# Gate/up by strip matmuls with early products, P·V ahead of the scores in a pass, and two row blocks of wo loaded before the last V page

## The chip, the cores and the metric

One Trainium2 chip; the kernel runs on one core. The core has a matrix engine (TensorE, PE in the profile; its weight loads are PEld), a vector engine (VectorE, DVE), a scalar engine (ScalarE, ACT), GpSimd (POOL), and SyncE (SP), which here issues every DMA of data. Each engine runs its own instruction stream; they meet at semaphores. The metric is the device time of one execution in microseconds, as the median of several runs.

## The reference

One token (`x`, 512 wide) goes through a grouped-query attention over a long cache and, beside it, through a gated feed-forward block; a scalar gate mixes the two:

```python
def reference(A_x, A_k_cache, A_v_cache, A_wq, A_wo, B_x, B_w_gate, B_w_up, B_w_down, gate_w):
    x = A_x                                              # [1, 1, 512]
    g = sigmoid((x * gate_w).sum(-1, keepdims=True))
    # attention: 32 query heads, 8 key/value heads, 32768 cached positions, head width 128
    q = x @ wq                                           # 512 x 4096
    p = softmax(q k^T * 128 ** -0.5)                     # 4 query heads share one key/value head
    a = (p v) @ wo                                       # 4096 x 512
    b = (silu(x @ w_gate) * (x @ w_up)) @ w_down         # 512 x 1792, 512 x 1792, 1792 x 512
    return g * a + (1 - g) * b
```

All inputs are bfloat16. The caches are 2 x 8 x 32768 x 128 values, 134 MB together.

## The kernel before, in words

**Storage.** SBUF holds three pages of one cache head each (`page`, 64 KB in each of 128 partitions, 8.39 MB in all). Pages 0 and 1 take the K heads in turn, page 2 the V heads. At the start page 2 holds `wq`, `w_gate` and `w_up` instead; at the end page 0 holds `w_down` and `wo`.

**The order of loads (SP, L331 to L357).** All loads of data are issued by SP in one order, and SP waits in that order too: `wq`, `x`, `gate_w`, `w_gate`, `w_up`, K0, K1; then for each j the load of K(j+1) (when its page's transposes are done, `sem_tr`) and of V(j) (V0 when gate/up is done, `sem_pe_h`; each later one when P·V of the head before has read the page, `sem_v_done`). After K7 and V6 come `w_down`, V7 in five pieces (each as V6's rows are used up), and `wo` in five pieces cut by `WO_CUTS` (in row blocks, 32 in all). SP then waits for the result row and stores it.

**Start (PE `emit_q`).** Four small matmuls turn `x` into columns (`xT`). 32 matmuls with one column of `xT` as the stationary operand give q as rows: four strips of the array at once, 512 columns each, into `ps_sc` (L381). Then gate and up: 112 matmuls (L398) whose stationary operand is a 128 x 128 piece of the weights and whose moving operand is one column of `xT`, in a loop of 2 x 7 turns of 8 matmuls; the result is two groups of 14 columns in `ps_c`. Then four matmuls (L410) spread the transposed q, from which VectorE builds `qblk`. VectorE reads q (L608) and transposes it (L613) while gate/up runs.

**Scores (S).** For each head VectorE transposes the K page in 32 units of 128 x 512 words into two slots (L672, `sem_tr`); TensorE works each unit off with 16 columns of q as the moving operand, 8 matmuls per unit (`emit_s`, L436, `sem_sc`). The two engines hand the two slots back and forth. At the end of a head VectorE takes the maximum (`pmax`, L681), GpSimd makes it global (L295), ScalarE forms the exponentials (L557) and rearranges them into `ET` (L570).

**P·V.** `emit_v` has 64 matmuls in four strips (L455) that read V's page; every eighth signals `sem_v_done`. ScalarE copies the result out (L566), four transposes (`emit_reduce`, L469) follow, and VectorE sums the diagonal blocks into `oT`.

**The pass loop.** TensorE has one hardware loop over passes p = 1 to 11. A pass does the scores of head p-1 and then, from pass 2 on, P·V of head p-2 with its reduction (`emit_v(p)`, `emit_reduce(p + 1)`). The order of work is so S0; S1, V0; S2, V1; and so on to S7, V6; then `w_down` (`emit_wd`, L482) and V7; then the output projection (`emit_wide`), and in the last pass the rest of `wo`. `emit_wide` takes the first 20 row blocks of `wo` in four strips of 512 columns (L501) into `ps_w`, and the others as pairs of 256 columns into `ps_c` (`emit_wo`, `emit_rows`, L230). VectorE copies `ps_w` to `part` (L735), two more pairs of matmuls add the strips of `part` into `ps_c`, and VectorE writes the row (L747).

**The gated product.** ScalarE takes the sigmoid of the gate (L543); VectorE forms the products and scales them by 1 - g in `emit_end`, after the scores of the last head (L697, L702, L704). `w_down` needs them.

## Time and profile before

| | |
|---|---|
| time, 3 runs | median 354.25 us (354.12 to 354.78) |
| profiled execution | 354.53 us, span 353.0 us |
| busy, share of the span | PE 51%, PEld 33%, DVE 53%, ACT 26%, POOL 2% |
| read from HBM | 148.11 MB, 420 GB/s over the span |
| longest waits of the DMA queue (SP) | for P·V (L455) 247.5 us, for gate/up (L398) 37.5, for the transposes (L672) 26.4 |
| gate/up, L398 | 15.9 us of matmul, from 18.07 to 41.24 us |
| chain that ended last | DMA 45%, DVE 21%, PE 21%, issue 11% |

The span runs from the first to the last instruction. The chain is followed back from the last instruction to what released it at each step; "issue" is time in which an engine waited for nothing that the profile shows, so its own stream (branches, register work). A line such as `L672 <-DMA ...` gives what ended the idle time of that line's engine. DMA's "us to landing" counts from the issue to the last semaphore signal.

### The profile page before, as it was taken

Reading aid. Unit: us, or ns where it says so; the run is one execution under the profiler, and the core shown is the slowest. Engines: PE = TensorE matmul, PEld = TensorE weight load, DVE = VectorE, ACT = ScalarE, POOL = GpSimd, SP = SyncE. Lnnn points to the kernel's source line nnn. Section 1 sums busy time; section 2 is a strip of 40 time slices with the busy share of each in tenths; the row PEclk is TensorE's granted clock in tenths of the full one; section 3 lists DMA queues with packets and bytes.
Section 4 is the critical chain, followed back from the end, with each engine's and each line's share of the span. In section 5 each row is a group of like instructions: output and inputs, shape, how many; then the busy total and the mean of one; then the engine's idle time right before and its main releaser. Section 6 shows DMA issues by size and latency. Waiting matters only on the chain.

```text
span 353.0 us, 7887 instructions
## 1 busy us (share of the span) xinstructions
PE 180.7 (51%) x2807; PEld 116.9 (33%) x2807; DVE 187.7 (53%) x307; ACT 92.5 (26%) x220; POOL 8.4 (2%) x29
## 2 busy tenths in 40 slices
PE   0466545445664580456625580556235575547745
PEld 0155434344434430344214430443124424422112
DVE  2020189889639930897049911995069818960001
ACT  1000100092173039000750048002810066024300
POOL 4000000000000000000000000000000000001000
PEclk9999999999985558555655567555855565556856
DMA  8998998998969999998998998998999999989996
GB/s 334 409 504 386 446 475 371 460 475 356 475 238 423 408 475 394 438 475 386 446 475 356 475 475 356 475 475 356 475 431 401 416 423 468 475 355 433 429 420 239
DMA packets 4330, 148.14 MB, mean 420 GB/s; under 512 B 484, under 2 KB 488, under 8 KB 1000
## 3 DMA queue, kind: packets, MB, share of 16 engines
q1 hardware_dynamic: 4328, 148.12, 97.7%
q8 instruction: 1, 0.02, 0.0%
q14 instruction: 1, 0.01, 0.0%
HBM read 148.11 MB, written 0.00 MB: 420 GB/s over the span
## 4 chain that ended last, share of the span: by engine, by line
DMA 45%; DVE 21%; PE 21%; issue 11%; SPq 1%; DVEq 1%; ACT 0%
DMA page<-in_A_k_cache_dram 27%; DVE slot L672 21%; PE ps_o L455 9%; DMA page<-in_A_v_cache_dram 8%; DMA page<-in_A_wo_dram 7%; PE ps_sc L436 6%; PE ps_c L398 5%; DMA E<-in_gate_w_dram 3%; PE ps_sc L381 1%; SPq L353 0%; DVE qblk L618 0%; SPq L307 0%; PE ps_o L469 0%; PE ps_c L230 0%; ACT acc L566 0%
## 5 line engine op out<-in xcount | busy, mean ns | idle before, releaser
L672 DVE STREAM_TRANSPOSE slot<-page 128x512 f32<-128x512 f32 x256 | 166.6, 691 | 89.1 <-DMA page<-in_A_k_cache_dram 67.8
L436 PE MATMUL ps_sc<-qcur,slot 128*128 128x16 bf16 x2048 | 96.0, 178 | 126.0 <-DVE slot L672 121.9
L436 PEld LDWEIGHTS ps_sc<-qcur,slot 128*128 128x128 bf16 x2048 | 77.1, 107 | 145.8 <-issue 143.9
L455 PE MATMUL ps_o<-page,ET 128*16 128x512 bf16 x512 | 48.4, 555 | 13.0 <-DMA page<-in_A_v_cache_dram 7.9
L570 ACT ACTIVATE ET<-E 32x256 bf16<-32x256 bf16 x128 | 52.8, 412 | 1.4
L552 ACT ACTIVATE nbias<-gmax 128x4 f32<-128x4 f32 x8 | 1.6, 205 | 178.4 <-POOL gmax L295 178.4
L455 PEld LDWEIGHTS ps_o<-page,ET 128*16 128x16 bf16 x512 | 17.0, 119 | 41.0 <-issue 28.0
L557 ACT ACTIVATE E<-ps_sc,nbias 128x256 bf16 x32 | 21.8, 850 | 1.8 <-ACT nbias L552 1.8
L398 PE MATMUL ps_c<-xT,page 128*128 128x1 bf16 x112 | 15.9, 217 | 8.0 <-issue 7.2
L398 PEld LDWEIGHTS ps_c<-xT,page 128*128 x112 | 14.4, 138 | 10.3 <-issue 9.9
L618 DVE CAST qblk<-ps_m 32x128 bf16<-32x128 f32 x4 | 1.1, 287 | 22.3 <-PE ps_m L410 22.1
L681 DVE TENSOR_REDUCE pmax<-ps_sc 128x4 f32<-128x1024 f32 x8 | 9.8, 1226 | 4.5 <-PE ps_sc L436 4.5
L552 ACT ACT_TABLE_LOAD x8 | 10.3, 1283 | 0.1
L721 DVE TENSOR_REDUCE oT<-ps_o 128x4 f32<-128x64 f32 x1 | 0.2, 224 | 18.5 <-PE ps_o L469 18.5
L295 POOL PARTITION_ALL_REDUCE gmax<-pmax x8 | 3.0, 373 | 297.8 <-DVE pmax L681 297.8
L566 ACT ACTIVATE acc<-ps_o 128x512 f32<-128x512 f32 x8 | 4.8, 606 | 16.6 <-PE ps_o L455 16.6
L557 ACT ACTIVATION_READ_ACCUMULATOR E<-ps_sc,nbias x32 | 9.1, 284 | 0.0
L469 PE MATMUL ps_o<-ident_f,acc 128*128 128x128 f32 x32 | 5.7, 305 | 5.6 <-ACT acc L566 4.9
L543 ACT ACTIVATE sg<-ps_c 128x14 f32<-128x14 f32 x1 | 0.2, 183 | 26.7 <-PE ps_c L398 26.7
L469 PEld LDWEIGHTS ps_o<-ident_f,acc 128*128 128x128 f32 x32 | 3.6, 150 | 10.1 <-ACT acc L566 8.4
L366 PE MATMUL ps_m<-eye,E 2*128 2x2 bf16 x4 | 0.3, 166 | 13.0 <-DMA E<-in_gate_w_dram 13.0
L482 PE MATMUL ps_w<-page,vec 128*1 x14 | 5.2, 514 | 1.4 <-issue 1.4
(61 smaller groups left out, 37.2 us busy)
## 6 DMA issues: line engine op xcount, KB each, us to landing
page<-in_A_k_cache_dram SPq DMA_DIRECT2D x2, 4096.0 KB, 42.5
page<-in_A_v_cache_dram SPq DMA_DIRECT2D x3, 2048.0 KB, 12.3
page<-in_A_wq_dram SPq DMA_DIRECT2D x1, 4096.0 KB, 12.3
page<-in_A_v_cache_dram SPq DMA_DIRECT2D x2, 1024.0 KB, 11.8
page<-in_A_wo_dram SPq DMA_DIRECT2D x1, 2048.0 KB, 22.1
page<-in_A_wo_dram SPq DMA_DIRECT2D x4, 512.0 KB, 24.1
page<-in_B_w_gate_dram SPq DMA_DIRECT2D x1, 1792.0 KB, 15.5
page<-in_B_w_up_dram SPq DMA_DIRECT2D x1, 1792.0 KB, 19.4
```

The source lines that it names most:

```text
L381: ins = pe.matmul(ps_sc[32 * s : 32 * s + 1, b * 512 : (b + 1) * 512], xT[:, c : c + 1], wq_v[:, c, g * 512 : (g + 1) * 512], start=(c == ...
L398: ins = pe.matmul(ps_c[:, bass.ds(w * FC + f * 2 + (C_G0 + e), 1)], gu_cols(at + f * 2 + (c * F + e)), xT[:, c : c + 1], start=(c == 0), s ...
L436: ins = pe.matmul(ps_sc[:, bass.ds(at[s * RPU + r], NS)], sv[:, s, r, e // 2, e % 2, :], qcur[:, e, :], start=(e == 0), stop=(e == JE - 1),)
L455: ins = pe.matmul(ps_o[32 * c : 32 * c + VW, :], ET[:, k * VW : (k + 1) * VW], rows(V_PAGE, n, n + RQ), start=(k < NSTRIP), stop=(k >= NT ...
L469: ins = pe.transpose(ps_o[:, q * 128 : (q + 1) * 128], acc[:, q * 128 : (q + 1) * 128], ident_f[:, :],)
L482: pe.matmul(ps_w[0:1, :], vec[:, bass.ds(n * 2 + c, 1)], page[:, bass.ds(n * (2 * NOUT) + (o0 + c * NOUT), NOUT)], start=False, stop=False ...
L552: act.activation(nbias[:, :], gmax[:, :], ACT.Copy, scale=-SCALE).then_inc(sem_nbias, 1)
L557: act.activation(ev[:, h, :, :], scv[:, h, :, :], ACT.Exp, bias=nbias[:, h : h + 1], scale=SCALE, accum_out=esum[:, bass.ds(j * HPG + h, 1 ...
L566: act.activation(acc[:, :], ps_o[:, :], ACT.Copy).then_inc(sem_acc, 1)
L570: ins = act.activation(etv[QP * i : QP * (i + 1), :, g, :], E[QP * g : QP * (g + 1), i * w : (i + 1) * w].rearrange("p (f m) -> p f m", f=KH),
L672: dve.transpose(slot_f[:, s * (SLOT // 2) : (s + 1) * (SLOT // 2)].rearrange("p (x g b) -> p g x b", g=NQ, b=QP), kp[:, f, :, tu * UW : (t ...
L681: dve.tensor_reduce(pmax[:, :], ps_sc[:, p * RB * NS : (p + 1) * RB * NS].rearrange("p (x h) -> p h x", h=HPG), AX.X, ALU.max,).then_inc(s ...
```

## The change

Gate and up are computed like q: 16 strip matmuls each, with a column of `xT` stationary and 448 columns of the weights moving, into the second half of `ps_sc`, whose memset now covers all of it. They come after L410, which gives `qblk`, and not before it. The sigmoid and the products are taken right there, 448 wide in four strips, then transposed into `tT`; V0's load waits for one signal from TensorE instead of 14. The semaphore presets of VectorE stand at its start instead of behind `qcur`.

In a pass P·V and its reduction come first, then the scores, then `w_down` or `emit_wide`. `emit_v(p - 1)` in pass p reads head p-3, so the order of all the work stays S0; S1; V0, S2; V1, S3; ... V6, `w_down`; V7, wide. The computed lists of the score loop are written out at their uses. The `w_down` loop does one matmul a turn instead of two.

`wo` has six pieces: row blocks 0 and 1 are loaded between `w_down` and V7, the others after V7; 24 blocks go the wide way, 4 follow in the same pass, and the matmuls with `part` and the last two pieces are in the last pass.

```diff
@@ -56,8 +56,8 @@
 
-    WO_CUTS = [0, 16, 20, 24, 28, 32]
-    KW = 2
+    WO_CUTS = [0, 2, 16, 24, 28, 30, 32]
+    KW = 3
     KL = 4
@@ -69,6 +69,7 @@
     EW = NT * HPG
+    FS = F // NQ
     KH = 2
@@ -145,7 +146,6 @@
         selz = T("selz", [128, SW], FP32)
-        sg = T("sg", [128, FC], FP32)
         res_row = T("res_row", [64, OW], BF16)
@@ -170,6 +170,9 @@
         q_blk = slot[:, 2 * RQ * DH : 4 * RQ * DH]
+        sg = acc[:, 0:FS]
+        t_row = slot[:, 0:FS]
+        t_blk = slot[:, D : D + FS]
         spread = ET[:, 0 : NSTRIP * 128].rearrange("p (s m) -> p s m", s=NSTRIP)
@@ -185,8 +188,7 @@
         M_O0 = M_P0 + JE * H
-        C_G0 = OW
-        assert C_G0 + 2 * FC <= 512
+        S_Q0, S_G0, S_U0 = 0, 1024, 1536
         assert M_O0 + WOJ <= 512
@@ -247,9 +249,6 @@
             return ins
-
-        def gu_cols(at):
-            return page[:, bass.ds(at, QP * NQ, step=FC)]
 
@@ -325,7 +324,7 @@
                     else:
-                        sp.wait_ge(sem_pe_h, FC)
+                        sp.wait_ge(sem_pe_h, 1)
                     cache(A_v_cache, j, V_PAGE).then_inc(sem_v, 16)
@@ -343,14 +342,18 @@
                 )
+                def load_wo(k):
+                    a, b = WO_CUTS[k], WO_CUTS[k + 1]
+                    src = A_wo.rearrange("(p j) n -> p j n", j=WOJ)
+                    sp.dma_start(wo_v[:, a:b, :], src[:, a:b, :]).then_inc(sem_wo[k], 16)
+
+                load_wo(0)
                 for k, sem in enumerate(sem_v7):
...
                     cache(A_v_cache, G - 1, V_PAGE, a, b).then_inc(sem, 16)
-                for k in range(len(sem_wo)):
-                    a, b = WO_CUTS[k], WO_CUTS[k + 1]
-                    src = A_wo.rearrange("(p j) n -> p j n", j=WOJ)
-                    sp.dma_start(wo_v[:, a:b, :], src[:, a:b, :]).then_inc(sem_wo[k], 16)
+                for k in range(1, len(sem_wo)):
+                    load_wo(k)
                 sp.wait_ge(sem_dve_row, 1)
@@ -387,22 +390,6 @@
                     ins.then_inc(sem_pe_q, 1)
-                    pe.sem_inc(sem_fu, 1)
-                    pe.wait_ge(sem_fg, 16)
-                    with pe.Fori(0, 2, 1) as w:
-                        pe.wait_ge(sem_fu, pe.compute_val(w * 16 + 1))
-                        at = pe.compute_val(w * (KC * F) + w1)
-                        with pe.Fori(0, FC // 2, 1) as f:
-                            for e in range(2):
-                                for c in range(KC):
-                                    ins = pe.matmul(
-                                        ps_c[:, bass.ds(w * FC + f * 2 + (C_G0 + e), 1)],
-                                        gu_cols(at + f * 2 + (c * F + e)),
-                                        xT[:, c : c + 1],
-                                        start=(c == 0),
-                                        stop=(c == KC - 1),
-                                    )
-                        ins.then_inc(sem_pe_h, 1)
                     pe.wait_ge(sem_const, 4)
@@ -415,6 +402,19 @@
                     ins.then_inc(sem_pe_qp, 1)
+                    for w, (sem, base) in enumerate(((sem_fg, S_G0), (sem_fu, S_U0))):
+                        pe.wait_ge(sem, 16)
+                        for c in range(KC):
+                            for s in range(NSTRIP):
+                                ins = pe.matmul(
+                                    ps_sc[32 * s : 32 * s + 1, base : base + FS],
+                                    xT[:, c : c + 1],
+                                    wgu[:, w, c, s * FS : (s + 1) * FS],
+                                    start=(c == 0),
+                                    stop=(c == KC - 1),
+                                    skip_group_check=True,
+                                )
+                    ins.then_inc(sem_pe_h, 1)
 
@@ -424,17 +424,17 @@
                     with pe.Fori(0, UNITS // SLOTS, 1) as u:
-                        n = [pe.compute_val(n0 + u * SLOTS + (s + 1)) for s in range(SLOTS)]
-                        at = [
-                            pe.compute_val(c0 + u * (SLOTS * RPU * NS) + x * NS)
-                            for x in range(SLOTS * RPU)
-                        ]
                         for s in range(SLOTS):
-                            pe.wait_ge(sem_tr, n[s])
+                            pe.wait_ge(sem_tr, n0 + u * SLOTS + (s + 1))
                             for r in range(RPU):
...
                                     ins = pe.matmul(
-                                        ps_sc[:, bass.ds(at[s * RPU + r], NS)],
+                                        ps_sc[
+                                            :,
+                                            bass.ds(
+                                                c0 + u * (SLOTS * RPU * NS) + (s * RPU + r) * NS, NS
+                                            ),
+                                        ],
                                         sv[:, s, r, e // 2, e % 2, :],
@@ -477,16 +477,15 @@
                     pe.wait_ge(sem_ld_wd, 16)
-                    with pe.Fori(0, FC // 2, 1) as n:
-                        for c in range(2):
-                            pe.matmul(
-                                ps_w[0:1, :],
-                                vec[:, bass.ds(n * 2 + c, 1)],
-                                page[:, bass.ds(n * (2 * NOUT) + (o0 + c * NOUT), NOUT)],
-                                start=False,
-                                stop=False,
-                                skip_group_check=True,
-                            )
+                    with pe.Fori(0, FC, 1) as n:
+                        pe.matmul(
+                            ps_w[0:1, :],
+                            vec[:, bass.ds(n, 1)],
+                            page[:, bass.ds(n * NOUT + o0, NOUT)],
+                            start=False,
+                            stop=False,
+                            skip_group_check=True,
+                        )
 
@@ -508,28 +507,24 @@
                     pe.wait_ge(sem_dve_oz, 1)
-                    emit_wo(pe, KW)
-                    pe.wait_ge(sem_dve_w, 1)
-                    emit_rows(pe, lambda e: selz[:, SW - 1 : SW] if e else selz[:, :], part, False)
-                    for k in range(KW + 1, KL):
-                        emit_wo(pe, k)
+                    emit_wo(pe, KW).then_inc(sem_late, 1)
 
...
                         arm()
+                        with pe.If(((p + (G - 3)) >> 3) == 1):
+                            emit_v(p - 1)
+                            emit_reduce(p)
                         with pe.If(p < G + 1):
...
                             emit_wd()
-                        with pe.If(p < G + 2):
-                            with pe.If(p > 1):
-                                emit_v(p)
-                                emit_reduce(p + 1)
                         with pe.If(p == G + 2):
...
                     with pe.Else():
-                        pe.sem_inc(sem_late, 1)
+                        pe.wait_ge(sem_dve_w, 1)
+                        emit_rows(pe, lambda e: selz[:, SW - 1 : SW] if e else selz[:, :], part, False)
                         for k in range(KL, len(sem_wo)):
@@ -539,8 +534,8 @@
                 act.activation(g_col[:, :], gtot[:, :], ACT.Sigmoid).then_inc(sem_act_g, 1)
-                act.wait_ge(sem_pe_h, FC)
-                act.activation(sg[:, :], ps_c[:, C_G0 : C_G0 + FC], ACT.Sigmoid).then_inc(sem_act_sg, 1)
+                act.wait_ge(sem_pe_h, 1)
+                act.activation(sg[:, :], ps_sc[:, S_G0 : S_G0 + FS], ACT.Sigmoid).then_inc(sem_act_sg, 1)
                 ev = E[:, :].rearrange("p (i r h) -> p h i r", h=HPG, i=NQ)
@@ -587,11 +582,17 @@
 
-                dve.sem_inc(sem_sc, SLOTS)
-                dve.memset(ps_sc[:, 0:1024], 0.0).then_inc(sem_psw, 1)
+                dve.memset(ps_sc[:, :], 0.0).then_inc(sem_psw, 1)
                 dve.memset(ps_c[:, :], 0.0).then_inc(sem_psw, 1)
...
                 dve.memset(ps_o[:, :], 0.0).then_inc(sem_v_done, VTURN)
+                dve.sem_inc(sem_sc, SLOTS)
+                for sem in sem_v7[1:] + [sem_k7, sem_acc]:
+                    dve.sem_inc(sem, 1)
+                dve.sem_inc(sem_red, 2)
+                dve.sem_inc(sem_ep, 1)
+                dve.sem_inc(sem_v, 16)
+                dve.sem_inc(sem_tr, UNITS)
                 xg = ps_m[:, M_X0 : M_X0 + 2 * KC].rearrange("p (c e) -> p e c", e=2)
@@ -626,14 +627,28 @@
                 dve.tensor_copy(qc, qblk[:, 0 : JE * NS])
+                dve.wait_ge(sem_act_sg, 1)
+                dchain(
+                    dve.tensor_scalar(og_col[:, :], g_col[:, :], -1.0, 1.0, op0=ALU.mult, op1=ALU.add)
+                )
+                dchain(dve.tensor_tensor(sg, sg, ps_sc[:, S_G0 : S_G0 + FS], ALU.mult))
+                dchain(
+                    dve.scalar_tensor_tensor(
+                        t_row.rearrange("p (j l) -> p j l", j=FC),
+                        sg.rearrange("p (l j) -> p j l", j=FC),
+                        og_col[:, 0:1],
+                        ps_sc[:, S_U0 : S_U0 + FS].rearrange("p (l j) -> p j l", j=FC),
+                        ALU.mult,
+                        ALU.mult,
+                    )
+                )
+                dchain(dve.transpose(t_blk, t_row))
+                dve.tensor_copy(tT, t_blk.rearrange("p (j l) -> p j l", j=FC)[:, :, 0]).then_inc(
+                    sem_dve_tT, 1
+                )
+                dve.wait_ge(sem_dve_tT, 1)
                 PF = PAGE // 2
                 UW = RPU * DH // 2
-                for sem in sem_v7[1:] + [sem_k7, sem_acc]:
-                    dve.sem_inc(sem, 1)
-                dve.sem_inc(sem_red, 2)
-                dve.sem_inc(sem_ep, 1)
-                dve.sem_inc(sem_v, 16)
-                dve.sem_inc(sem_tr, UNITS)
 
@@ -692,23 +707,6 @@
                 def emit_end():
-                    dve.wait_ge(sem_act_sg, 1)
-                    dchain(
-                        dve.tensor_scalar(
-                            og_col[:, :], g_col[:, :], -1.0, 1.0, op0=ALU.mult, op1=ALU.add
-                        )
-                    )
-                    dchain(
-                        dve.tensor_tensor(sg[:, :], sg[:, :], ps_c[:, C_G0 : C_G0 + FC], ALU.mult)
-                    )
-                    dve.scalar_tensor_tensor(
-                        tT,
-                        sg[:, :],
-                        og_col[:, 0:1],
-                        ps_c[:, C_G0 + FC : C_G0 + 2 * FC],
-                        ALU.mult,
-                        ALU.mult,
-                    ).then_inc(sem_dve_tT, 1)
                     dve.wait_ge(sem_red, G + 1)
@@ -733,6 +731,7 @@
                     dve.tensor_copy(part[:, :], ps_w[:, :]).then_inc(sem_dve_w, 1)
+                    dve.wait_ge(sem_late, 1)
 
@@ -742,7 +741,6 @@
                     with dve.Else():
-                        dve.wait_ge(sem_late, 1)
                         dve.wait_ge(sem_pe_sum, 1)
```

## The prediction

> **What bounds the kernel now.** I read the page first, for bytes and rate, then the busy time in stretches, to see where the rate is not held.
>
> ```profile
> q1 hardware_dynamic: 4328, 148.12, 97.7%
> HBM read 148.11 MB, written 0.00 MB: 420 GB/s over the span
> ```
>
> ```profile
> 60.00:90.00 30.00, 14.74 (x312) 11.94 (x312) 26.87 (x43) 11.07 (x27) 0.38 (x1) 1.00 0.97 419
> 90.00:110.00 20.00, 12.66 (x189) 7.22 (x188) 10.79 (x17) 11.33 (x27) 0.37 (x1) 0.84 0.86 357
> 110.00:150.00 40.00, 18.62 (x324) 12.16 (x324) 22.56 (x37) 11.30 (x27) 0.37 (x1) 0.59 0.98 424
> 150.00:230.00 80.00, 39.01 (x680) 25.69 (x680) 46.80 (x74) 22.61 (x54) 0.74 (x2) 0.56 1.00 433
> ```
>
> The last two columns are the share of the DMA engines and GB/s. Full rate is 433, and 148.12 MB at 433 is 342.1 us of a 353.0 us span. So the kernel is bound by loading; only the other 11 us can be won, and one stretch, 90 to 110, is short of rate. The DMA queue's timeline and the landing times say why:
>
> ```profile
> 41.27 0.33 SPq L307 DMA_DIRECT2D page<-in_A_v_cache_dram  x1
> 67.97 0.33 SPq L307 DMA_DIRECT2D page<-in_A_k_cache_dram  x1
> 100.79 0.33 SPq L307 DMA_DIRECT2D page<-in_A_v_cache_dram  x1
> 101.16 0.43 SPq L307 DMA_DIRECT2D page<-in_A_k_cache_dram  x1
> ```
>
> ```profile
> page<-in_A_k_cache_dram SPq DMA_DIRECT2D x1, 31.0
> ```
>
> ```profile
> page<-in_A_v_cache_dram SPq DMA_DIRECT2D x1, 21.8
> ```
>
> The K load issued at 67.97 lands 31.0 later, at 98.97, and nothing is queued behind it: V1 is issued at 100.79 and lands 21.8 later, at 122.6. One cache page is 8.39 MB, 19.4 us at 433 GB/s, so right behind the K page V1 would have landed at 118.4. **The hole costs 4.2 us.** Every later issue comes with a backlog: V2 is issued at 132.26 while the load of 101.16 lands only at 142.0 (40.8 after its issue). What held V1 back is in the chain, and in the timeline of the first scores:
>
> ```profile
> 93.38 0.81 issue
> 94.20 6.58 PE ps_o L455 x64
> 100.80 0.61 ACT acc L566
> 101.45 0.66 PE ps_o L469 x4
> 102.11 1.37 issue
> ```
>
> ```profile
> 41.27 0.18 ACT L543 ACTIVATE sg<-ps_c 128x14 f32<-128x14 f32 x1 [26.67 <-PE ps_c L398]
> 42.02 1.25 DVE L618 CAST qblk<-ps_m 32x128 bf16<-32x128 f32 x4 [22.15 <-PE ps_m L410]
> 45.20 2.61 DVE L672 STREAM_TRANSPOSE slot<-page 128x512 f32<-128x512 f32 x4 [1.71 <-issue]
> 48.06 2.65 DVE L672 STREAM_TRANSPOSE slot<-page 128x512 f32<-128x512 f32 x4 [0.25 <-PE ps_sc L436]
> ```
>
> V1's page is free when V0's 64 matmuls end at 100.8; these follow the scores of groups 0 and 1, which start at 45.20. K0 was there earlier: the two K loads issued at 2.79 have a median landing of 47.6 and the later one 57.0, so K0 took 38.2 and landed at 41.0. The start waited for gate/up (L398, to 41.24, 112 matmuls at 217 ns and a loop turn of 0.5 us after each 8), then L410, qblk, and 1.71 us of DVE semaphores and registers.
>
> **Gate/up by strips.** L381 does the same kind of work: 32 strip matmuls of 512 columns in 3.58 us, 0.112 each. The change has 16 for gate and 16 for up, 448 columns: 1.8 us each. Up lands at 2.22 + 19.4 = 21.6 (issue row), so they end near 23.5; L410 and qblk now come before them. The products on ACT and DVE are 448 wide: from L608 and L613 (1024 wide, 1.23 and 1.25) about 0.6 for each of three wide steps, 0.6 for the sigmoid, 0.5 for two narrow ones: done by 27. K0's landing at 41.0 covers that by 14 us; without the cover it would be 3 us. The larger memset (0.9 us more at 1.1) lies under the wait for x until 13. V0 is issued at 24 rather than 41.27, behind K1 either way: nothing.
>
> So group 0 starts at K0's landing plus the DVE's registers between wait and first transpose, 0.4 us: 41.4, **3.8 us earlier**.
>
> **V first, scores second.** The order of work on PE stays S0, S1, V0, S2, V1 and so on; what moves is the loop's turn. Before, it lies between V and the next S (1.37 of issue, with the score loop's own set-up); after, between S and the next V (0.81), and V is what frees V1's page. The trace's branch records put the turn (counter, back branch, tests, hint) at about 0.8, a jump over the wide block adds 0.25: V0 starts 1.05 later after S1. Bounds: 0 and 1.37, the whole of the other gap. In later passes V's end has 6 us to spare (V2 above: 9 us before the backlog is gone).
>
> **The score loop** loses its two computed lists, and the wait and the address are worked out where used. No row shows the new form. Two ends: a unit takes 0.717 (2.87 per 4 transposes) and its transpose 0.655, so at best it gains 0.062 x 64 = 4.0 us before V0; at worst each unit gets one more register instruction with its issue, 0.1 (0.04 to 0.05 for one in the trace, as much between two), 6.4 us. I take 0: L398's loop also writes its address out for each matmul, and its trace has one register instruction per address and none for a repeated one, so the count hardly changes.
>
> V1 is then issued at 100.79 - 3.8 + 1.05 = 98.0 and lands at 119.8 instead of 122.6: **-2.8 us**. All later loads stand behind it in one queue, so all move.
>
> **wo and the tail.** Two of 32 rows come before V7 (0.26 MB, 0.6 us, 0.7 with the slower small packets), so V7's last piece lands 0.7 later against the end of loading. Total bytes are unchanged. Before, PE waited 0.6 for the last wo piece:
>
> ```profile
> 350.70 0.28 PE L230 MATMUL ps_c<-page,slot 128*32 128x256 bf16 x1 [0.61 <-DMA page<-in_A_wo_dram]
> ...
> 351.42 0.42 DVE L747 CAST res_row<-ps_c 64x256 bf16<-64x256 f32 x1 [2.95 <-PE ps_c L230]
> ```
>
> After, PE must do 24 rows wide (20 x 0.107 + 0.16 = 2.3 before), then rows 24 to 28, a loop turn of 1.2 (348.9 to 350.4 in the trace), then the part rows (0.86) and 4 rows (0.6). Counted from V7's last landing: wo 16 to 24 lands at +6.8, rows 24 to 28 at +8.1, Else reached at +9.4, part rows done +10.3, end +10.9 to +11.3; before it was +10.9. So the tail loses 0.7 from V7 and 0 to 0.4: **+0.75**, bounds 0.2 and 1.2. PE, not the last load, ends it. The loop of w_down (L482) turns 14 times instead of 7, each turn some 0.6 in place of 0.8 for two: 8.4 us for 5.5, with V7's first matmul at 334.7 instead of 330.9 on the old scale. V7's fourth piece lands at 338.6 and the last at 341.1, and 40 matmuls at 0.107 fit before the former: covered, by 0.4 us at the slow matmul rate.
>
> One more DMA and smaller ones: the five wo loads landed from 323.15 + 22.1 to 325.06 + 25.6, four of 0.52 MB in 5.4 us, 1.35 each against 1.21 at 433. So an extra piece costs 0.14 (0 to 0.4), in the 0.75. The Trainium skill, "DMA: Bandwidth & Descriptors", Bandwidth, wants DMAs of 1 MiB or more and fits a fixed 2.0 us to each (for another issue path); by that the extra piece would make the sum nearly zero. The row shows that queued pieces do not pay it.
>
> **Sum:** -2.8 + 0.75 = -2.05. The profiled execution took 354.53 for its span of 353.0, 0.3 above the median of 354.25; from the median, **352.2**. A measurement of this kernel can tell 0.2%, 0.7 us, from no change.
>
> **Rivals.** *The hole closes whole.* If the turn is hidden or the score loop gains 0.02 per unit, V1 is issued by 96.6: -4.2 + 0.6 gives 350.6. For: the 0.25 the DVE waits for PE after four transposes. Against: the moved turn. 0.20.
>
> *The register work lands on the score loop, slower.* At 0.1 per unit V0 ends 6.4 later, V1 is issued at 104.4, the hole grows by 3.6, with the tail +4.35: 358.6. It decides from 0.03 per unit on (2.05 / 64), where gain and tail cancel. For: PE idles 0.56 to 0.65 per loop turn before DVE's data, so it is near the edge. Against: L398's records. Later passes have room for 3.2 us. 0.10.
>
> *It does not start earlier*: something else holds the first transposes, or the turn costs all of 1.37 and more, and only the tail and a small gain are left: 353.5 to 355. For: DVE has semaphore work before its loop, but that now ends before 41. 0.12.
>
> *The tail eats it*: w_down's turn at 0.75 instead of 0.6 pushes V7 by 14 x 0.15 - 0.4 = 1.7 us, 353.9; or the added small load pays what V1 paid over its data, 21.8 - 19.4 = 2.4: 354.6. For the second there is V1's row, against it the 1.35 of the queued pieces. 0.06. The page of the Trainium skill named above states such a fixed price per DMA; the rows of the queued wo pieces do not agree with it.
>
> **Numbers.** Forecast (351 to 353.5) 0.52. Faster by over 0.2%: 0.52 + 0.20 and a part of the rest, 0.75; within: 0.10, from the last two; slower: 0.10 and a part of these, 0.15. The range 350.4 to 354.3 holds the forecast, nearly all of the first rival and most of the last two: 0.8. The forecast's own range is 351 to 353.5.
>
> **What would show it.** Right: first L672 near 41.4; L398's group gone and 64 strip matmuls before 24; V1's issue near 98 and landing near 120; 0.717 per score unit; PE idle before L455 near 1.9 and before the next scores near 0.5; last PE group not waiting for wo. Wrong: V1 issued after 100, a unit over 0.75, V7 waiting for w_down's loop instead of its own piece, or a new stretch under 430 GB/s after 110.

## The result and the profile after

The changed kernel takes **352.25 us** (median of 10 runs, 351.68 to 353.85) against 354.11 for the kernel before on the same chip (10 runs, 352.88 to 354.99): ratio 0.9954, 95% interval 0.9937 to 0.9972. The forecast was 352.2. The profiled execution took 352.33 with a span of 350.8; before, 354.53 with 353.0. So the span shows the gain in full: 2.2 us. Ratios here are of undisturbed runs alone, so they can differ from the quotient of two medians; three of the start alone's twelve runs below count as disturbed, and with them its median would be 356.40.

First the busy time in stretches, as before (last two columns: share of the DMA engines and GB/s):

```profile
60.00:90.00 30.00, 15.41 (x308) 12.12 (x312) 26.66 (x42) 11.28 (x28) 0.75 (x2) 1.00 0.97 419
90.00:110.00 20.00, 12.03 (x181) 6.86 (x174) 10.13 (x16) 11.09 (x27) 0.00 (x0) 0.78 0.99 419
110.00:150.00 40.00, 19.81 (x332) 12.91 (x332) 22.57 (x37) 11.32 (x27) 0.37 (x1) 0.59 1.02 441
150.00:230.00 80.00, 41.20 (x680) 26.62 (x676) 46.99 (x76) 22.66 (x54) 0.74 (x2) 0.56 1.00 433
```

The stretch 90 to 110, at 357 GB/s before, is now at 419. The timeline of SP's DMA queue and the time from V1's issue to the landing of its last DMA engine:

```profile
23.77 0.33 SPq L306 DMA_DIRECT2D page<-in_A_v_cache_dram  x1
63.35 0.33 SPq L306 DMA_DIRECT2D page<-in_A_k_cache_dram  x1
95.73 0.33 SPq L306 DMA_DIRECT2D page<-in_A_v_cache_dram  x1
96.11 0.43 SPq L306 DMA_DIRECT2D page<-in_A_k_cache_dram  x1
```

```profile
page<-in_A_v_cache_dram SPq DMA_DIRECT2D x1, 23.6
```

V1 is issued at 95.73 instead of 100.79. By the trace's landing records, one for each of the 16 DMA engines, K2 lands from 98.45 (first engine) to 98.97 (last), and V1 from 118.0 to 119.38; before it was 122.05 to 122.57. The last engine counts, so 3.2 of the 4.2 us of the hole are closed. But the engines are now 1.38 apart, where they were 0.52 apart. That spread is still there at the last wo landing (345.65 to 347.14).

The start, in the timeline of PE and DVE:

```profile
20.57 3.15 PE L409 MATMUL ps_sc<-page,xT 128*1 128x448 bf16 x32
23.77 0.55 ACT L538 ACTIVATE acc<-ps_sc 128x448 f32<-128x448 f32 x1 [8.95 <-PE ps_sc L409]
26.88 0.18 DVE L646 COPY vec<-slot 128x14 bf16<-128x14 bf16 x1
41.29 6.85 DVE L687 STREAM_TRANSPOSE slot<-page 128x512 f32<-128x512 f32 x10 [14.24 <-DMA page<-in_A_k_cache_dram]
```

Gate, up and their products end at 27.1; the first transposes wait for K0 and nothing else. V0 and the end of the kernel:

```profile
89.88 5.81 PE L455 MATMUL ps_o<-page,ET 128*16 128x512 bf16 x64 [1.83 <-issue]
...
100.24 0.92 PE L431 MATMUL ps_sc<-qcur,slot 128*128 128x16 bf16 x16 [3.19 <-DVE slot L687]
```

```profile
349.16 0.42 DVE L745 CAST res_row<-ps_c 64x256 bf16<-64x256 f32 x1 [2.75 <-PE ps_c L232]
349.61 0.27 SPq L358 DMA_DIRECT2D out_dram<-res_row  x1
```

The loop's turn now stands in front of V0 (1.83 of issue for 0.81). The cast comes 2.0 us after the last wo landing (349.16 against 347.14); before it was 0.8 (351.42 against 350.65).

### The profile page after: what moved, and what is told of

Its sections match the earlier page's. It is cut to its first block, busy times and chain, and to the rows that moved or that the text cites. A ratio compares the mean times of both kernels' runs of the same rounds, so it can differ in the third digit from the quotient of the medians.

```text
span 350.8 us, 7554 instructions
## 1 busy us (share of the span) xinstructions
PE 174.7 (50%) x2723; PEld 106.3 (30%) x2723; DVE 190.8 (54%) x309; ACT 92.9 (26%) x220; POOL 8.3 (2%) x29
## 4 chain that ended last, share of the span: by engine, by line
DMA 63%; PE 15%; DVE 14%; issue 7%; SPq 1%; DVEq 0%
DMA page<-in_A_k_cache_dram 48%; DVE slot L687 13%; DMA page<-in_A_v_cache_dram 8%; DMA page<-in_A_wo_dram 7%; PE ps_sc L431 7%; PE ps_o L455 7%; PE ps_c L232 1%; SPq L306 0%; SPq L348 0%; SPq L334 0%; DVE oT L675 0%; DVEq L683 0%; DVE res_row L745 0%; DVEq L666 0%; SPq L330 0%
## 5 line engine op out<-in xcount | busy, mean ns | idle before, releaser
L431 PE MATMUL ps_sc<-qcur,slot 128*128 128x16 bf16 x2048 | 103.5, 179 | 126.9 <-DVE slot L687 113.4
L431 PEld LDWEIGHTS ps_sc<-qcur,slot 128*128 128x128 bf16 x2048 | 80.9, 107 | 151.0 <-issue 150.1
L455 PE MATMUL ps_o<-page,ET 128*16 128x512 bf16 x512 | 46.8, 541 | 21.0 <-issue 12.3
L455 PEld LDWEIGHTS ps_o<-page,ET 128*16 128x16 bf16 x512 | 16.1, 117 | 48.2 <-issue 34.5
L552 ACT ACTIVATE E<-ps_sc,nbias 128x256 bf16 x32 | 21.8, 851 | 1.7 <-ACT nbias L547 1.7
```

The source lines that it names most:

```text
L431: ins = pe.matmul(ps_sc[:, bass.ds(c0 + u * (SLOTS * RPU * NS) + (s * RPU + r) * NS, NS),], sv[:, s, r, e // 2, e % 2, :], qcur[:, e, :], ...
L455: ins = pe.matmul(ps_o[32 * c : 32 * c + VW, :], ET[:, k * VW : (k + 1) * VW], rows(V_PAGE, n, n + RQ), start=(k < NSTRIP), stop=(k >= NT ...
L552: act.activation(ev[:, h, :, :], scv[:, h, :, :], ACT.Exp, bias=nbias[:, h : h + 1], scale=SCALE, accum_out=esum[:, bass.ds(j * HPG + h, 1 ...
```

## The experiments

Each kernel was timed against the kernel before on the same chip. The kernel before had medians of 353.96 there in the first set, 353.72 in the second and 354.53 in the third. Only one execution of each kernel is profiled, so a time quoted from a trace belongs to that execution and not to the median.

### First set: the parts of the change

In these expectations theory A is the prediction's: what counts is when V1 is issued. Theory B, its rival, puts the gain into the score loop and its written-out lists. Each text states what it expects of them.

**The start alone.** The kernel before with gate/up by strips, early products and presets, nothing else:

```diff
-                    with pe.Fori(0, 2, 1) as w:
...
+                    for w, (sem, base) in enumerate(((sem_fg, S_G0), (sem_fu, S_U0))):
+                        pe.wait_ge(sem, 16)
...
-                        sp.wait_ge(sem_pe_h, FC)
+                        sp.wait_ge(sem_pe_h, 1)
```

> The kernel before with one part of the change: gate/up by strips, products and semaphore presets early; pass order, score loop, w_down loop and wo stay as before. Theory A (one hole in the load queue is the whole gain): scores of group 0 start at 41.3 instead of 45.2, V1 is issued at 100.8 - 3.9 = 96.9, the hole of 4.2 us shrinks to about 0.3 and the tail pays nothing: 350.2 to 351.1 against 354.1 before, better than the whole change. Theory B (the gain is engine work saved in every pass: score loop and V first): the start lies under loads and 353.8 to 354.1 results.

Measured: 355.72 (352.48 to 357.23, 9 runs), ratio 1.003, 0.9994 to 1.0066: no gain. Both theories missed. The profiled execution is a fast one, at 354.26; what made others slower still, no trace shows. The transposes do start at 41.23, but V1 is issued only at 96.79 and lands from 118.34 to 120.66. And a second gap opens ahead of the last V block, which the timeline of the queue and the stretches show:

```profile
287.59 0.43 SPq L342 DMA_DIRECT2D page<-in_B_w_down_dram  x1
315.68 5.66 SPq L306 DMA_DIRECT2D page<-in_A_v_cache_dram  x5
```

```profile
310.00:318.00 8.00, 4.90 (x68) 2.39 (x72) 3.09 (x5) 2.98 (x9) 0.73 (x2) 0.50 0.75 297
318.00:324.00 6.00, 4.13 (x42) 1.46 (x34) 0.73 (x3) 2.98 (x8) 0.60 (x2) 0.78 1.01 360
```

V7's first piece is issued at 315.68, when `w_down`, the last load in the queue, lands from 316.56 on. The piece lands 4.25 us after `w_down` on the last engine (323.08 against 318.83). Before, with the piece issued at 317.29 and `w_down` landing at 320.08 to 320.45, it was 2.75. A load that comes earlier at the first hole lets the queue run empty earlier at the next place where a load has little lead.

A third delay in this trace has nothing to do with a short lead. From 47.37 to 48.40 a packet of 16 KB of instructions goes over a DMA engine (q8, instruction, in the profile's table of DMA queues). The load that is under way then is K1, and one engine lands it at 61.45, the other fifteen by 60.20. That engine is still late at K2 (100.16 against 98.97 in the change).

**All but the start.** The changed kernel with gate/up, products and presets as before:

```diff
-                    for w, (sem, base) in enumerate(((sem_fg, S_G0), (sem_fu, S_U0))):
...
+                    with pe.Fori(0, 2, 1) as w:
```

> The changed kernel with the old start (gate/up by 112 matmuls ahead of L410, products at the end, presets late), all else changed. Theory A: V1 is issued at 95.7 + 3.9 = 99.6, the hole is still 3 us, and the tail costs its 1.0: 353.5 to 354.1. Theory B: about 352.2, as the whole change.

Measured: 354.29 (353.59 to 354.99), ratio 1.0007, 0.9992 to 1.0023. That is 0.2 above theory A's range and 2 above theory B's 352.2: V1 is issued at 99.69, 3.3 us of the hole stay, and without the earlier start the rest of the change brings nothing.

**wo as before.** The changed kernel without the two row blocks ahead of V7:

```diff
-    WO_CUTS = [0, 2, 16, 24, 28, 30, 32]
-    KW = 3
+    WO_CUTS = [0, 16, 20, 24, 28, 32]
+    KW = 2
```

> The changed kernel with wo as before: five pieces (16, 4, 4, 4, 4), all after V7, the part matmuls in the wide pass. Theory A (the tail cost about 1.0: 0.65 because two row blocks stand ahead of V7, the rest because PE and not the last load ends the kernel): 351.2, the last PE group again waits for wo. Rival (the tail is decided by the last load wherever the pieces are cut): 352.2, no difference.

Measured: 352.96 (351.49 to 353.74), ratio 0.9966, 0.9949 to 0.9984. Missed. The tail is shorter, as expected: the cast comes 0.76 after the last wo landing instead of 2.0. But in this trace K0 already lands 1.3 late on its last engine (40.41 to 42.24), V1 is issued at 97.22 and its last engine lands at 121.19, which takes more than the tail gave. Here the packet of instructions goes from 25.78 to 26.80, while K0 is loaded: fifteen engines land K0 by 40.85 and one at 42.24. So it is in all three kernels that have the new start and the old pieces of wo; in the other traces that packet comes only after 347, and K0 and K1 end within 0.7. The times fit; no run tests the packet by itself.

**The lists computed.** The changed kernel with the score loop's two computed lists:

```diff
+                        n = [pe.compute_val(n0 + u * SLOTS + (s + 1)) for s in range(SLOTS)]
+                        at = [
...
-                            pe.wait_ge(sem_tr, n0 + u * SLOTS + (s + 1))
+                            pe.wait_ge(sem_tr, n[s])
```

> The changed kernel with the score loop's two computed lists back. Theory A: the unit is 0.717 instead of 0.69, V1 is issued 1.4 us later, at 97.1, and the hole reopens by 0.5 at most: 352.2 to 352.7. Theory B (score loop time counts in each of eight heads): 0.7 to 0.9 us for each head, 357 to 359.

Measured: 354.07 (352.33 to 355.65), ratio 0.9997, 0.9973 to 1.0021. The gain is gone, which is more than A allowed and far less than B did. V0 starts at 91.05 for 89.88, and V1 is issued at 96.83.

### What these left open: how early is early enough

In three of these four traces V1 was issued before the queue ran dry, and yet it landed late. From the landing records of one execution of each kernel, for these and for the kernels of the later sets: the lead, by which V1's issue precedes the first engine's end of K2; how far apart the engines finish V1; and the loss, V1's last landing less K2's last landing less the 19.4 us of a page at full rate.

| kernel | V1 issued | lead | V1 spread | V1's last landing | loss |
|---|---|---|---|---|---|
| before | 100.79 | -2.1 | 0.52 | 122.57 | 4.2 |
| all but the start | 99.69 | -1.2 | 0.66 | 121.65 | 3.3 |
| before, V in halves | 97.96 | 0.5 | 0.48 | 119.64 | 1.1 |
| start and wo | 97.81 | 0.8 | 0.75 | 119.81 | 1.4 |
| wo as before | 97.22 | 1.4 | 2.59 | 121.19 | 1.2 |
| start alone | 96.79 | 1.6 | 2.32 | 120.66 | 1.1 |
| lists computed | 96.83 | 1.7 | 2.15 | 120.53 | 2.0 |
| scores first | 95.98 | 2.4 | 1.59 | 119.78 | 1.6 |
| the change | 95.73 | 2.7 | 1.38 | 119.38 | 1.0 |
| the change once more | 95.82 | 3.1 | 0.92 | 119.24 | 0.6 |
| part rows in the pass | 95.14 | 3.2 | 0.64 | 118.37 | -0.1 |
| V in halves, old wo | 94.92 | 3.5 | 1.95 | 119.80 | 0.0 |
| V in halves | 93.51 | 5.0 | 0.49 | 118.43 | 0.0 |
| V in halves, part rows in the pass | 93.41 | 5.0 | 0.51 | 118.37 | 0.0 |

For V in halves the issue and the spread are those of the first half, the last landing and the loss those of the second. In the three kernels with the early packet of instructions (wo as before, start alone, V in halves with the old wo) most of the spread is older than V1: K2's engines already end 1.96, 1.75 and 1.96 apart. The loss counts from K2's last engine and leaves that out.

From the first rows came theory C: the hole is what costs, but its edge is not sharp. A load issued less than some 3 us before the queue runs dry loses time on some of the DMA engines, and where the queue never runs dry again, that lag stays to the end. The two row blocks of wo are then worth something as lead for V7. The whole table agrees on the 3 us: from 3.2 us of lead on nothing is lost, at 3.1 it is 0.6. Between 0.5 and 2.7 the loss is 1.0 to 2.0 without an order in it, so the lead alone does not give its size.

### Second set

**The change once more**, as the measure for this set:

> The changed kernel once more, beside the kernel before and the variants on the same chip. 352.2 to 352.6 against 354.0. Theory C (a load must be issued some 3 us before the queue runs out, else the slowest DMA engine loses time): V1 issued near 95.7, its last engine lands 23.7 later, at 119.4. Theory A (a hole with a sharp edge at 96.6): V1 lands at 118.4 on all engines.

Measured: 352.39 (351.07 to 354.28), ratio 0.9972, 0.9952 to 0.9992; V1 issued at 95.82, landed at 118.32 to 119.24, by theory C's 119.4 and not theory A's 118.4.

**V in two halves.** The changed kernel; each V page is loaded in two halves, the first as soon as its half of the page has been read, and V7 gets a sixth piece by a cut at its middle:

```diff
+                        sp.wait_ge(sem_v_done, VTURN * j + VH // (RQ * VB))
+                        cache(A_v_cache, j, V_PAGE, 0, VH).then_inc(sem_v, 16)
...
-                    cache(A_v_cache, j, V_PAGE).then_inc(sem_v, 16)
+                        cache(A_v_cache, j, V_PAGE, VH, NT).then_inc(sem_vh, 16)
```

> The changed kernel with each V page loaded in two halves, the first one issued when the P.V of the head before has read the first half of the page. Theory C: V1's first half is issued near 92.8, so with over 5 us of lead; its landings spread by 0.5 us again instead of 1.4, all later loads move up by 0.9: 351.3 and a narrower scatter. Theory A: the hole was closed already, 352.2 as the whole change.

Measured: **351.94 (351.78 to 352.30, 5 runs)**, ratio 0.9956, 0.9943 to 0.9968. That lies between theory C's 351.3 and theory A's 352.2, and the interval overlaps that of the change (0.9952 to 0.9992); it is the landings that agree with theory C. The queue and the stretches:

```profile
63.32 0.33 SPq L308 DMA_DIRECT2D page<-in_A_k_cache_dram  x1
93.51 2.96 SPq L308 DMA_DIRECT2D page<-in_A_v_cache_dram  x2
96.51 0.44 SPq L308 DMA_DIRECT2D page<-in_A_k_cache_dram  x1
```

```profile
110.00:150.00 40.00, 20.78 (x340) 13.45 (x340) 23.50 (x39) 11.31 (x27) 0.37 (x1) 0.54 1.00 433
```

The engines stay 0.5 or less apart from K2 to the last wo landing (346.06 to 346.43), and the runs lie within 0.5 us of each other, against 3.2 for the change (12 runs).

**Start and wo.** The kernel before with the new start and the new pieces of wo; order of a pass and lists as before. The diff is that of the start alone, and

```diff
-    WO_CUTS = [0, 16, 20, 24, 28, 32]
+    WO_CUTS = [0, 2, 16, 24, 28, 30, 32]
```

> The kernel before with the new start and the new wo pieces, two row blocks ahead of V7; scores first, computed lists and w_down's double turn stay. Theory C: the start alone gave 356.4 because the first piece of V7 was issued 0.9 us before the fast engines ran out; the two row blocks give 0.65 us of lead there, so 353.0 to 354.0, better than the start alone in spite of the longer tail. Theory A: the wo pieces cost 1.0 on top: 357.

Measured: 353.96 (352.12 to 354.91), ratio 0.9999, 0.9981 to 1.0018: theory C's range. With two row blocks of wo ahead of it, V7's first piece lands 2.48 after them, and the second gap is gone:

```profile
310.00:318.00 8.00, 5.24 (x60) 2.18 (x64) 2.09 (x4) 3.00 (x9) 1.23 (x3) 0.50 0.99 413
318.00:324.00 6.00, 3.61 (x37) 1.26 (x25) 0.72 (x3) 4.09 (x10) 0.00 (x0) 0.93 1.02 432
```

**Scores first.** The changed kernel with the old order in a pass:

```diff
-                        with pe.If(((p + (G - 3)) >> 3) == 1):
-                            emit_v(p - 1)
-                            emit_reduce(p)
...
+                        with pe.If(p < G + 2):
+                            with pe.If(p > 1):
+                                emit_v(p)
+                                emit_reduce(p + 1)
```

> The changed kernel with the old order in a pass (scores, then P.V). The loop's turn goes back to its place behind P.V: V0 starts 1.0 us earlier, V1 is issued at 94.7. Theory C: 0.5 to 0.9 faster than the whole change, 351.3 to 351.8, with a smaller spread of V1's landings. Theory A: no difference, 352.2.

Measured: 352.48 (352.00 to 353.99), ratio 0.9976, 0.9959 to 0.9992: no difference from the change (352.39). The turn goes back to 0.90 of issue, but the score loop is 1.4 slower than in the change (48.2 for 46.8 from the first transpose to its end), so V0 starts 0.3 later and V1 is issued at 95.98. Theory C's 351.3 to 351.8 was built on V1 issued at 94.7, which did not come, so this run does not test it.

### Third set

**V in halves and nothing of the change**, on the kernel before. The diff is that of V in two halves.

> The kernel before, and one edit of my own: each V page is loaded in two halves, the first issued as soon as the products have read the first half of the page. Nothing of the change is in it. Theory (a load must be in the queue some 3 us before the queue runs dry, then the hole of 4.2 us closes): the first half of V1 is issued at 97.5 to 98, 0.5 before the queue runs dry, not 3, so most of the hole closes but the slowest DMA engines still lose 1 to 1.5 us: 351.3 to 352.5 us, against 353.7 to 354.0 for the kernel before. Rival (the earlier start and the new score loop are needed, and the issue of V1 is not what costs): 353.5 to 354.2, no difference.

Measured: **352.09 (351.45 to 352.50)**, ratio 0.9933, 0.9912 to 0.9955. The rival is out: one edit at the queue gives what the whole change gives, with gate/up, order, lists and wo untouched. In the traces all of it lies before V1's landing (122.57 to 119.64); from there to the cast it takes 229.43, where it was 228.85.

```profile
41.32 0.81 SPq L309 DMA_DIRECT2D page<-in_A_v_cache_dram  x2
97.96 2.36 SPq L309 DMA_DIRECT2D page<-in_A_v_cache_dram  x2
100.36 0.44 SPq L309 DMA_DIRECT2D page<-in_A_k_cache_dram  x1
```

The first half is issued 0.5 before K2's first engine ends (98.50). Its last landing is 109.95, where it is 108.72 with five us of lead. K2's last engine ends 0.1 later here, so 1.1 of the hole is left, as theory C said. In one point C erred: the loss falls on all engines here (spread 0.46), not on the slowest.

**Halves, and the part rows in the pass; and the part rows alone.** The matmuls with `part` moved from the last pass into the pass of the wide blocks, once on V in halves, once on the change:

```diff
+                    pe.wait_ge(sem_dve_w, 1)
+                    emit_rows(pe, lambda e: selz[:, SW - 1 : SW] if e else selz[:, :], part, False)
...
-                        pe.wait_ge(sem_dve_w, 1)
-                        emit_rows(pe, lambda e: selz[:, SW - 1 : SW] if e else selz[:, :], part, False)
```

> The changed kernel with V pages in two halves, and the part matmuls of the last rows moved inside the pass over wo's wide blocks, so that no turn of a loop lies between the last wo landing and the part matmuls. If the new tail's 0.9 us is partly the loop's turn: 0.3 to 0.5 us under the version with V halves alone (351.9), so 351.4 to 351.6. If the tail is only the matmuls that run behind the last landing: no difference, 351.8 to 352.0.

> The changed kernel with the part matmuls moved inside the pass over wo's wide blocks, nothing else. Turn of the loop on the path: 0.3 to 0.5 us under the changed kernel (352.3): 351.8 to 352.0. Turn hidden by the landing of the last pieces: no difference, 352.2 to 352.5.

Measured: 352.15 (351.94 to 352.25), ratio 0.9936, 0.9916 to 0.9956; and 353.29 (351.92 to 354.22), ratio 0.9965, 0.9947 to 0.9982. Both came out above their expectations. The first kernel was timed on another chip than V in halves, so neither the times (352.15 and 351.94) nor the ratios (0.9936 and 0.9956) set the two apart. In the traces there is no gain: from V1's landing to the end of the span it takes 232.0 for 231.6, and in the second kernel 231.8 for the change's 231.4. Yet the row is cast sooner, as the end of the timeline of the second one shows:

```profile
347.54 0.42 DVE L745 CAST res_row<-ps_c 64x256 bf16<-64x256 f32 x1 [2.37 <-PE ps_c L232]
347.98 0.27 SPq L358 DMA_DIRECT2D out_dram<-res_row  x1
```

The cast is 1.6 after the last wo landing (345.95) instead of 2.0; but the span ends at 350.2, that is 2.2 after the row's store was issued, where it is 1.1 in the change. The store has landed at 349.10 (350.72 in the change), so it is not what the end waits for. TensorE's own records say what is: its last weight load starts at 346.87, and it reaches the end of its program at 349.89, where all engines meet. In the change these are 348.48 and 350.31. So what this edit takes off the matmuls is for the most part given back by TensorE's way out. The packet of instructions goes with it: it ends at 348.52 here and at 348.84 in the change, and in all eight traces with the new start and the new pieces of wo TensorE reaches its end 1.28 to 1.49 after it. That TensorE waits for these instructions is an inference from the times; no run tests it. For the second kernel the median is above the profiled execution's 351.92 by 1.4, with V1's lead at the edge; whether the slower runs lose at V1 is not known, since they have no trace.

**Halves with the old wo.** V in two halves on the change, with `WO_CUTS` as before (the diff of wo as before):

> The changed kernel with V pages in two halves and with the pieces of wo as before (none ahead of the last V block). If the two row blocks ahead of the last V block serve only as lead for its first piece, and the lead is the halves' already: tail 0.9 us shorter, 351.0 to 351.2. If the last V block's first piece, behind w_down, still is issued too late (as where the start alone was changed: 4.25 us instead of 2.45): 352 to 353.5.

Measured: **351.61 (351.39 to 352.09)**, ratio 0.9922, 0.9901 to 0.9943, the lowest of all. That is 0.5 under halves with the part rows (352.15) on the same chip, less than the 0.9 hoped for: here too the packet of instructions comes at 25.78 and K0's last engine lands late (40.29 to 42.25), and all later loads carry that spread. With the halves V7 needs no blocks of wo ahead of it (its first piece lands 2.47 after `w_down`); they only lengthen the tail. This version beats the kernel before. Against the change, which was timed on other chips, its interval (0.9901 to 0.9943) still overlaps that of the first ten runs (0.9937 to 0.9972) a little, and against the halves on the kernel before (0.9912 to 0.9955) it is not set apart.

## Why the prediction was right, and where it was not

**The mechanism: right.** The hole behind K2 was the thing to win, and the halves on the kernel before show it alone. V1's last landing was forecast at 119.8 and came at 119.38. From one profiled execution to the other the cast moved by -3.19 (V1's landing) + 0.93 (from there to the cast) = -2.26, where the sum was -2.8 + 0.75 = -2.05.

**Start: right.** -3.91 (45.20 to 41.29) for -3.8. The 32 strips took 3.15 us for 3.6, the products ended at 27.1 for 27.

**The turn between S and V: right in size** (+1.02 for +1.05), **but the score loop, taken as 0, was mis-sized.** This is the step that failed. The reason given was that the count of register instructions hardly changes. That much is so: between 60 and 80 us TensorE has some 7.4 of them for each turn of 16 matmuls, before and after. But the loop became faster all the same, by 1.43 us before V0, so the count was not what decided. From the first transpose to V0's start, scores and turn together:

| start | lists | order | kernel | us |
|---|---|---|---|---|
| old | computed | scores first | before | 49.0 |
| old | written out | V first | all but the start | 48.9 |
| new | computed | scores first | start alone; start and wo | 50.3; 50.2 |
| new | written out | scores first | scores first | 49.1 |
| new | computed | V first | lists computed | 49.6 |
| new | written out | V first | the change | 48.6 |

The six further traces with the change's front part, up to V0, give 48.5 to 48.7, so these differences are not scatter.

Behind the new start the written-out lists gain 1.1 to 1.2 in either order, and V first gains 0.5 to 0.7 with either lists, its longer turn included; but the new start makes the old loop 1.2 to 1.3 slower. TensorE's wait for the transposes in each turn of the score loop tells it in the timelines: 0.45 to 0.50 in the change, 0.53 with scores first, 0.56 to 0.61 before, 0.64 in the start alone. Two turns, before and in the change:

```profile
61.95 0.77 PE L436 MATMUL ps_sc<-qcur,slot 128*128 128x16 bf16 x16 [0.56 <-DVE slot L672]
```

```profile
61.57 0.93 PE L431 MATMUL ps_sc<-qcur,slot 128*128 128x16 bf16 x16 [0.46 <-DVE slot L687]
```

Why the same loop takes longer behind another start, and by what the written-out lists gain, is open. Without lists and order, the start would have been worth 2.7 at V0, not 3.8.

**V0's 64 matmuls** were taken at the 6.58 of the trace of before; the change's trace has 5.81, and traces of one front part range from 5.21 to 6.22; the kernel before with V in halves, whose front part is the old one, has 5.62. So the 0.77 lies within the scatter between executions and is no gain of the change; the sum had no term for it. All together V1's issue moved by -3.91 + 1.02 - 1.43 (score loop) - 0.77 = -5.09, measured -5.06, where -2.8 was forecast.

**The landing** came out right through a second error. The first rival says that the hole closes whole if V1 is issued by 96.6. It was issued at 95.73 and the hole did not close whole; it kept 1.0 us. What was missing is the lead: the table of leads shows no loss at 3.2 us and 1.0 at 2.7. V1 was issued 2.3 us earlier than forecast and took 23.65 to its last landing instead of 21.8; of these 1.85 us, 0.8 is the wait behind K2 (118.4 at the earliest) and 1.0 the lag. The two errors nearly cancelled: that the landing was met this closely is luck.

**wo and the tail: right.** From V1's last landing to the cast it took 228.85 before and 229.78 after: +0.9 for +0.75, in its bounds (its own terms, 0.7 and 0 to 0.4, add up to 0.7 to 1.1). TensorE and not the last load ends the kernel, as forecast: the loads end 0.3 sooner after V1 (227.8 for 228.1), the cast 1.25 later after them. `w_down`'s loop took 7.4 for 8.4 and stayed covered.

**The extra piece:** the piece of wo with four row blocks lands 1.28 after the piece ahead of it, the last two, with two row blocks each, 0.64 and 0.62: two half pieces take no longer than one whole one, so its price is 0 for the 0.14 taken. The Trainium skill, "DMA: Bandwidth & Descriptors", Anatomy of one DMA, fits a fixed cost of about 2.0 us to each DMA on another issue path; the queued pieces here do not agree with it as a cost per piece.

**The rivals.** Slower register work (from 0.03 per unit on) did not come: a unit takes 0.69 for 0.717. The start did begin earlier, and the tail ate little more than its term. But the value of wo's pieces was missed: the prediction counted them only as a cost in the tail, and they were also lead. Without them V7's first piece landed 4.25 after the load ahead of it in the start alone, with them 2.48 after it in start and wo.

## What to carry over

Where loads bound a kernel, count the lead of every load against the moment at which the first DMA engine runs dry, read its landing at the slowest one, and ask which place is next once one hole is closed. Where one engine alone is late, look for a packet of instructions among the data. A buffer that is freed in parts can be loaded in parts: one such edit gave as much here as four rewritten stages, and the runs with it lie closer together (within 0.3 to 1.1 us; 2.2 to 3.2 for the change). At the end, look at when each engine reaches the end of its program and not only at the last useful instruction.

## What the runs showed of the hardware

A lag that some of the DMA engines picked up stayed with them for 230 us (spread 1.38 at V1, 1.49 at the last wo piece, in the change). It shrank where the other engines had to wait for a load: with wo as before, from 2.60 at `w_down` to 1.45 at V7's first piece, issued 0.6 before the first engine was through with `w_down`. The profile's time to landing is that of the last engine; how far the others are ahead, only the 16 landings show.

A load of 16 KB of instructions in the middle of the data loads went with one engine landing 1.25 to 1.47 behind the other fifteen in three traces of three (wo as before, start alone, V in halves with the old wo), and with none in the eleven where it came after 347.

The granted clock between 60 and 88 us is 1.00 in some executions and 0.50 in others. These lines are of the kernel before and of the start alone (column before the DMA share):

```profile
60.00:88.00 28.00, 13.60 (x288) 11.02 (x288) 25.09 (x41) 11.07 (x27) 0.38 (x1) 1.00 0.96 412
```

```profile
60.00:88.00 28.00, 13.65 (x288) 11.18 (x288) 24.51 (x40) 11.07 (x27) 0.38 (x1) 0.50 0.96 414
```

The mean clock of a run tells the two kinds apart (about 0.60 and 0.71). What the low clock costs differs from kernel to kernel. With the lists computed the median is 354.85 (7 runs) at the low one and 352.71 (5) at the high one, with the part rows in the pass 353.69 (8) and 352.33 (4), for the change once more 352.96 (7) and 352.12 (5). But the change's first ten runs show nothing (352.24 in 6, 352.25 in 4), nor does wo as before (352.92 in 7, 353.10 in 5) or V in halves (351.89 in 2, 351.94 in 3). So it is neither the clock alone nor the clock with V1's lead; what decides is open. Nor does the score stage tell: start and wo at 1.00 takes as long for it as the start alone at 0.50 (50.2 and 50.3).
